# Six staging buffers and one weight piece per step in the expert stage of a fused attention and mixture-of-experts kernel

## Chip, cores and metric

The kernel runs on one core of a Trainium2 chip. Its time is the device time of one execution in microseconds (us), and the number to predict is the median over several executions. "Profile" means the page and the views made from one execution that the hardware profiler recorded.

## The reference, cut to what matters

Three stages follow each other. Attention with a running decay gives 2304 rows of 512 numbers. A dense feed-forward network works on them, and an expert stage on its result.

```python
scores = scale * q @ k.T + decay           # causal, 4 x 8 heads, S = 576, D = 64
x = softmax(scores) @ v                    # as 2304 x 512
h = x @ w_in                               # 512 -> 2048
x = maximum(0.01 * h, h) @ w_out           # 2048 -> 512
logits = x @ w_gate                        # 8 experts
# greedy over all logits in falling order: each token takes the first
# expert that still has room, each expert takes 2304 / 8 = 288 tokens
for e in range(8):
    h = maximum(x[mask[e]] @ w1[e], 0.0)   # 512 -> 1024
    out[mask[e]] = h @ w2[e]               # 1024 -> 512
```

## The kernel before, in words

**Products.** Every float32 product is made of three passes of a shorter format: a number is split into a high part (a cast) and a low part (the number less its high part), and high x high, low x high and high x low are added up in PSUM. So each operand costs a cast, mostly on ACT, and a subtraction on DVE or POOL before PE can use it. In the names, `h` at the end is a high part, `l` a low part: `gh` and `gl` for the hidden layer of the dense network, `eh` and `el` for that of an expert; `wh` stands for both parts of a weight.

**Stages.** Attention runs to about 300 us. The dense network's first product and half of its second follow, to about 438. Its second product, `deferred`, is put off: 9 groups of 256 tokens, each of 8 pieces of `g`, are multiplied from 438 on in the gaps of the routing, whose small steps (`r_...`, mostly on DVE) are one long dependent chain. `split_g` (L457, L458) splits a piece: the cast on ACT, the subtraction on POOL, and for the last group (number 8) the cast on ACT and the subtraction on DVE through helpers that keep the order of the program. After each group `leave_first` (L1012) copies the two sums `acc` to `xo`, which SP stores to `x2d` in memory. Rows for expert 0 are gathered there before the last group is finished; the rows that are missing then are added by products of the last sums `Y` with a selection matrix, in the PSUM banks `q_ct`, `q_base` and `q_misc`. `part_operand` (L1032, L1033) splits the result to `X0`, which the profile calls `XE`.

**Expert stage.** It begins at about 676.7. For each expert, `first` (L1172) makes one 128-row block of the hidden layer, 12 products of 128x288 into a bank `h3`; ACT makes `eh` (L1176) and DVE `el` (L1177). `after` (L1185) multiplies the block by a part of `w2`, 12 products into four banks `y`. One such step is j, and there are 8; block j+1 is made before the y products of step j. `turn` (L1163) transposes the gathered rows `xe` of the next expert into bank `T3` in four of the steps, and `leave` (L1192) transposes the result of the expert before, which POOL scatters to `out` with an indirect DMA (`send`, L1198).

**Weights.** An expert has 8 pieces of 512 KB: pieces 0 to 3 hold `w1`, pieces 4 to 7 `w2`. `split_weights` (L354 to L364) loads a piece with two DMAs on SP into a staging buffer `wst`, casts its two halves to `wh` and subtracts for the low parts. There are two staging buffers, and room for 10 split pieces (`WB` = 40 tiles). `fetch(e)` calls it for all 8 pieces of an expert, and is called for expert e+1 at the start of expert e. Pieces 0 to 3 of expert 0 are loaded during `deferred`.

**What sets the order.** A scheduler of the tile framework places the instructions of each engine from a simulated timeline, with the order of the program as its guide. Instructions through the lower-case helpers `vec`, `act`, `pe`, `gp`, `sp` (L74) are kept in program order on their engine, as are the y products of expert 0. All else, written with V, A, PE, G, may move.

**The end** (L1235 to L1240): the last result is transposed into four banks; 384 columns of each of three tiles are copied by DVE, ACT, DVE, and then DVE copies the last 128 columns of each, and POOL sends it.

Of the kernel before, what the change touches and what calls it, by code (L numbers as in the profile page):

```python
# [32 lines left out]
NC = DM // 128  # L33
# [13 lines left out]
FIN = ("act", "vec"), ("vec", "gp")  # L47
LAG = 3
AFTER = 1500, 800
WIDE1 = (0, 1), (2, 3), (4, 5), (6, 7), (8,)  # L50
# [179 lines left out]
def tile_kernel(ctx, tc, q, k, v, f, w_in, w_out, w_gate, w1, w2, out):  # L230
# [124 lines left out]

    def split_weights(pieces, lo_on, hi_on=A):
        st = wp.tile([128, 1024], FT, name="wst", tag="wst", bufs=2)
        for lo, hi, src in pieces:
            nc.sync.dma_start(st[:, lo:hi], src)
        r = []  # L360
        for u in range(2):
            r.append([wp.tile([128, 512], FR, name="wh", tag="w", bufs=WB) for _ in range(2)])
            x = st[:, 512 * u:512 * u + 512]
            hi_on.copy(r[u][0], x)  # L364
            lo_on.tensor_tensor(r[u][1], x, r[u][0], op=OP.subtract)
        return r
# [608 lines left out]
    def deferred(mm, last):  # L975

        for g in range(NG):
# [6 lines left out]
            def taken(half, i):  # L984
                if half:
                    x = gtp.tile([128, 2, GT], FT, name="g0", tag="g0", bufs=3)
                    nc.sync.dma_start(x, gd[g][:, 2 * i:2 * i + 2])
                else:
                    x = g1((g,), slice(2 * i, 2 * i + 2))[:, 0]
                return split_g(x, *((vec, act) if g == NG - 1 else (G, A)))  # L990
            ahead = []
# [45 lines left out]
    with ExitStack() as c2:  # L1037
# [95 lines left out]
        for t in range(2):  # L1133
            A.copy(Y[:, t, 0], last[t])
            V.tensor_tensor(Y[:, t, 1], last[t], Y[:, t, 0], op=OP.subtract)
        for l in range(2):
            for t in range(2):
                for c in range(NC):
                    mm(px[c][:, :CAP], Y[:, t, l, 128 * c:128 * c + 128], sel8[t], start=False, stop=l == t == 1)
# [5 lines left out]

    with ExitStack() as c3:
        ps = c3.enter_context(tc.tile_pool(name="ps3", bufs=1, reuse_waits="tile", space=PSUM))
        ep = c3.enter_context(tc.tile_pool(name="ep", bufs=1, reuse_waits="tile"))
        scat = []
        NJ = F2 // 128  # L1150

        def fetch(e):

            w = early if e == 0 else []
            for n in range(len(w) // 2, NC + NF // 2):
                w += split_weights(piece(e, n), vec, act if e == 0 and n < 6 else A)
            wa, wb = [w[:NC], w[NC:2 * NC]], w[2 * NC:]
            return wa, wb

        def turn(X, xe, c, own=False):  # L1160
            p = ps.tile([128, 512], FT, name="T3", tag="T3", bufs=2)
            for t in range(3):
                (pe if own else PE).transpose(p[:, M * t:M * t + M], xe[t][:, 128 * c:128 * c + 128], ident[:M, :M])  # L1163
            part_operand(X, c, p)

        def first(X, wa, j, own=False):
            h = ps.tile([128, 512], FT, name="h3", tag="h3", bufs=2)
            n = 0
            for x in range(2):
                for c in range(NC):  # L1170
                    for w in wa[j // 4][c][:2 - x]:
# [17 lines left out]
        def leave(e, ys, t):  # L1189
            p = ps.tile([128, 512], FT, name="T3", tag="T3", bufs=2)  # L1190
            for c in range(NC):
# [12 lines left out]
        def operand():  # L1204
            return ep.tile([128, NC, 2, CAP], FR, name="XE", tag="XE", bufs=2)
        W = {0: fetch(0)}
        xe = {}
# [3 lines left out]
        for e in range(E):  # L1211
            wb = W[e][1]
            if e + 1 < E:
                W[e + 1] = fetch(e + 1)
                xe[e + 1] = gather(e + 1, [ep.tile([M, DM], FT, name="xe", tag="xe", bufs=6) for _ in range(3)])
                X[e + 1] = operand()
            yt = [ps.tile([128, 512], FT, name="y", tag="y", bufs=NC) for _ in range(NC)]
            for j in range(NJ):
                for i in range(j, j + 2):
                    n, i = e + i // NJ, i % NJ  # L1220
                    if n < E and (n, i) not in g:
                        g[n, i] = first(X[n], W[n][0], i, e == 0)
                after(yt, wb, j, *g[e, j], e == E - 1, e == 0)
                if ys and j < 3:
# [5 lines left out]
            for c in range(NC):  # L1230
                (A.copy if c % 2 else V.tensor_copy)(ys[:, c], yt[c][:, :CAP])
        p = [ps.tile([128, 512], FT, name=n, tag=n, bufs=2) for n in ("T3", "T3", "h3", "h3")]
        for c in range(NC):
# [3 lines left out]
        for t in range(3):  # L1237
            (A.copy if t % 2 else V.tensor_copy)(yo[t][:, :384], p[t][:M, :384])
        for t in range(3):
            V.tensor_copy(yo[t][:, 384:], p[3][:M, 128 * t:128 * t + 128])  # L1240
            send(E - 1, yo[t], t)
# [226 lines left out]
```

## Time and profile before

| | |
|---|---|
| median of 3 runs | 921.39 us (920.62 to 921.4) |
| the profiled execution | 920.77 us, span of the trace 918.7 us |
| PE busy | 882.8 us, 96% of the span, 6916 instructions |
| DVE, POOL, ACT busy | 584.6, 440.3, 415.7 us |
| costliest group of PE | `acc` products of `deferred`, 185.5 us for 576 of them |
| `h` and `y` products of the experts with high parts | 101.1 us for 660, 100.8 us for 512 |
| casts of weights on ACT in the expert stage | 75.9 us for 124, with 80.9 us of idle time before them, most of it behind loads of `wst` |

Times in the trace count from the start of the span. A row gives a start, a duration and an instruction, `x` a count, and in brackets how long its engine stood idle before it and what ended that. An engine's idle time matters only where that engine, at that point, sets when the next work ends. The granted clock is TensorE's: 1.00 is its upper level of 2.4 GHz, about 0.5 the lower one of 1.2 GHz.

### The profile page before, as it was taken

The numbers are of one execution on the slowest core, as the hardware profiler recorded it, in microseconds if no ns is written. First come the engines' busy times: TensorE is split into PE (matmuls) and PEld (weight loads), VectorE is DVE, ScalarE is ACT, GpSimd is POOL, SyncE is SP. The second block draws the span as 40 slices with busy tenths as digits, with TensorE's granted clock in tenths as the row PEclk, the third lists the DMA queues.
The fourth block names the chain that finished last, engine by engine and source line by source line (L and its number), as shares of the span: only waits on it lengthen the run. The fifth ranks groups of instructions, "written<-read, shape, count | busy, mean of one in ns | idle before, by whom it ended". The sixth has DMA issues, their size and how long they took to land.

```text
span 918.7 us, 19048 instructions
## 1 busy us (share of the span) xinstructions
PE 882.8 (96%) x6916; PEld 751.6 (82%) x6916; DVE 584.6 (64%) x1458; ACT 415.7 (45%) x984; POOL 440.3 (48%) x670
## 2 busy tenths in 40 slices
PE   6899999999999999999999999999997999999996
PEld 6688878878878887776777777777787999999995
DVE  8778876517798379324867667776546665656631
ACT  7999999842223233314122222221345455555521
POOL 8588895548998078002656555554121122121111
PEclk9899999999999999999999999999999999999998
DMA  6566654559984485402321212212166665655601
GB/s 129 150 166 169 182 131 128 174 155 360 326 272 149 143 261 170 136 25 69 116 71 46 68 60 69 69 47 70 54 195 201 191 195 174 200 191 187 200 28 35
DMA packets 139965, 132.34 MB, mean 144 GB/s; under 512 B 68480, under 2 KB 106688, under 8 KB 139872
## 3 DMA queue, kind: packets, MB, share of 16 engines
q1 hardware_dynamic: 135600, 121.40, 43.1%
q0 software_dynamic: 3072, 9.44, 3.5%
q8 instruction: 54, 0.88, 0.4%
q10 hardware_dynamic: 1200, 0.30, 0.2%
q14 instruction: 39, 0.32, 0.1%
HBM read 99.84 MB, written 31.08 MB: 143 GB/s over the span
## 4 chain that ended last, share of the span: by engine, by line
PE 77%; POOL 7%; ACT 5%; DVE 3%; DMA 3%; issue 2%; POOLq 0%; SPq 0%; DVEq 0%; ACTq 0%
PE acc L1095 21%; PE h L74 11%; PE acc L74 11%; PE y L1185 10%; PE h L1172 10%; PE s L74 6%; PE T L74 3%; ACT kept L74 3%; DMA wst<-in_moe_w 2%; PE q_ct L1095 2%; POOL ln L74 2%; POOL wsq L74 2%; POOL P L74 1%; PE T L1192 1%; DVE r_ge L1346 1%
## 5 line engine op out<-in xcount | busy, mean ns | idle before, releaser
L1095 PE MATMUL acc<-wh,gh 128*128 128x512 f32 x576 | 185.5, 399 | 1.2 <-ACT gh L74 1.2
L458 POOL TENSOR_TENSOR gl<-g,gh 128x512 fp32r<-128x512 f32 x64 | 106.9, 1676 | 75.5 <-ACT gh L457 69.8
L74 DVE TENSOR_TENSOR wh<-wst,wh 128x512 fp32r<-128x512 f32 x144 | 99.0, 707 | 48.9 <-ACT wh L364 38.0
L1095 PEld LDWEIGHTS acc<-wh,gh 128*128 128x128 f32 x576 | 106.1, 189 | 20.3 <-ACT gh L74 1.6
L1095 PE MATMUL acc<-wh,gl 128*128 128x512 f32 x288 | 115.6, 402 | 1.3 <-POOL gl L458 1.3
L364 ACT CAST wh<-wst 128x512 fp32r<-128x512 f32 x124 | 75.9, 620 | 80.9 <-DMA wst<-in_moe_w 59.5
L74 PE MATMUL h<-X,wh 128*128 128x512 f32 (+1 forms) x480 | 104.2, 374 | 0.6 <-DVE xt L74 0.6
L74 PE MATMUL acc<-X,wh 128*128 128x512 f32 (+1 forms) x480 | 104.5, 374 | 0.0
L457 ACT CAST gh<-g 128x512 fp32r<-128x512 f32 x64 | 39.5, 621 | 142.8 <-PE acc L1095 120.4
L1172 PE MATMUL h<-XE,wh 128*128 128x288 f32 x660 | 101.1, 301 | 2.6 <-DVE el L1177 2.6
L1185 PE MATMUL y<-eh,wh 128*128 128x288 f32 x512 | 100.8, 297 | 2.7 <-ACT eh L1176 2.7
L74 PEld LDWEIGHTS h<-X,wh 128*128 128x128 f32 x480 | 82.5, 188 | 18.2 <-issue 1.0
L74 PEld LDWEIGHTS acc<-X,wh 128*128 128x128 f32 x480 | 82.3, 188 | 18.4 <-DVE g L74 1.7
L1172 PEld LDWEIGHTS h<-XE,wh 128*128 128x128 f32 x660 | 90.3, 189 | 2.8 <-DVE el L1177 2.8
L74 ACT ACTIVATE kept<-kept,nm 128x192 f32<-128x192 f32 (+4 forms) x160 | 88.0, 553 | 3.1 <-DVE nm L74 3.1
L1198 POOL DMA_INDIRECT out<-yo,ids x24 | 24.0, 1002 | 127.6 <-DVE yo L1194 103.9
L1185 PEld LDWEIGHTS y<-eh,wh 128*128 128x128 f32 x512 | 81.0, 189 | 3.2 <-ACT eh L1176 3.2
L74 DVE SCALAR_TENSOR_TENSOR wbits<-w,wbits 128x256 int32<-128x256 int32 x128 | 73.3, 575 | 2.3
L74 DVE CUSTOM_DVE_ANT_0 kept<-s,mask 128x192 f32<-128x192 f32 (+4 forms) x160 | 59.2, 426 | 22.7 <-PE s L74 22.0
L1185 PE MATMUL y<-el,wh 128*128 128x288 f32 x256 | 70.5, 299 | 0.5 <-DVE el L1177 0.5
L1027 POOL DMA_INDIRECT xe<-x2d,ids x24 | 26.1, 1089 | 93.6 <-PE T L1163 34.8
L74 POOL TENSOR_TENSOR wst<-wsq,wbits 128x256 f32<-128x256 f32 x64 | 50.6, 791 | 33.0 <-DVE wbits L74 28.2
(245 smaller groups left out, 1731.4 us busy)
## 6 DMA issues: line engine op xcount, KB each, us to landing
wst<-in_moe_w SPq DMA_DIRECT2D x128, 256.0 KB
X<-xd SPq DMA_DIRECT2D x12, 1024.0 KB
g<-gd SPq DMA_DIRECT2D x36, 256.0 KB
w<-in_moe_w_in SPq DMA_DIRECT2D x32, 256.0 KB
w<-in_moe_w_out SPq DMA_DIRECT2D x32, 256.0 KB
gd<-g SPq DMA_DIRECT2D x16, 512.0 KB
xd<-xt SPq DMA_DIRECT2D x16, 320.0 KB
x2d<-xo SPq DMA_DIRECT2D x20, 256.0 KB
```

The source lines that it names most:

```text
L74: r = getattr(self.engine, name)(*a, **k)
L364: hi_on.copy(r[u][0], x)
L457: hi_on.copy(gh, g)
L458: on.tensor_tensor(gl, g, gh, op=OP.subtract)
L1027: G.indirect_dma_start(out=x, out_offset=None, in_=x2d[:, :], in_offset=bass.IndirectOffsetOnAxis(ap=ids[:, 3 * e + t:3 * e + t + 1], axis=0))
L1095: tc.keep_in_program_order(PE.matmul(*a, **k))
L1172: (pe if own else PE).matmul(h[:, :CAP], w[:, 128 * (j % 4):128 * (j % 4) + 128], X[:, c, x, :], start=n == 0, stop=n == 3 * NC - 1)
L1185: o = PE.matmul(yt[c][:, :CAP], w[:, s], a, start=j == 0 and n == 0, stop=j == NJ - 1 and n == 2)
L1192: PE.transpose(p[:M, 128 * c:128 * c + 128], ys[:, c, M * t:M * t + M], ident)
L1198: sd = G.indirect_dma_start(out=out[:, :], out_offset=bass.IndirectOffsetOnAxis(ap=ids[:, 3 * e + t:3 * e + t + 1], axis=0), in_=y, in_off ...
L1346: V.scalar_tensor_tensor(many[:, :NT * (K + 1)].rearrange("p (i k) -> p i k", k=K + 1)[:, :, :K], key[:, :, None].to_broadcast(s), base if ...
```

## The change

1. `split_weights` takes a room: with one, the piece is staged in one of `NWS` = 6 buffers `ws` of the experts' own pool. Only pieces 4 and 5 of expert 0 still use `wst`.
2. `fetch` becomes `more(e, n)`, one piece, called once in every inner step: an expert's own pieces 6 and 7 in its steps 0 and 1, the next expert's pieces 0 to 5 in steps 2 to 7. All casts and subtractions keep the order of the program.
3. The PSUM pool of the experts becomes three, with `h3` first. `h3` so lies in banks of the last `acc`, and no longer in those of `q_ct`.
4. In `deferred`, the first two pieces of the last group are split by instructions that may move. The very first piece of group 0 has its low part made on DVE, not on POOL.
5. The products with `Y` go tile by tile instead of high parts first.
6. At the end each tile's copies stand together, and ACT makes the 384-column copies of two tiles.

```diff
+NWS = 6
...
-    def split_weights(pieces, lo_on, hi_on=A):
-        st = wp.tile([128, 1024], FT, name="wst", tag="wst", bufs=2)
+    def split_weights(pieces, lo_on, hi_on=A, room=None):
+        st = room.tile([128, 1024], FT, name="ws", tag="ws", bufs=NWS) if room else wp.tile([128, 1024], FT, name="wst", tag="wst", bufs=2)
...
-                return split_g(x, *((vec, act) if g == NG - 1 else (G, A)))
+                n = NF // 2 * half + i
+                return split_g(x, *((vec, act) if g == NG - 1 and n > 1 else (V if g == NG - 1 or g == n == 0 else G, A)))
...
-        for l in range(2):
-            for t in range(2):
+        for t in range(2):
+            for l in range(2):
                 for c in range(NC):
                     mm(px[c][:, :CAP], Y[:, t, l, 128 * c:128 * c + 128], sel8[t], start=False, stop=l == t == 1)
...
+        psh = c3.enter_context(tc.tile_pool(name="ps3h", bufs=1, reuse_waits="tile", space=PSUM))
+        pst = c3.enter_context(tc.tile_pool(name="ps3t", bufs=1, reuse_waits="tile", space=PSUM))
         ps = c3.enter_context(tc.tile_pool(name="ps3", bufs=1, reuse_waits="tile", space=PSUM))
...
-        def fetch(e):
-
-            w = early if e == 0 else []
-            for n in range(len(w) // 2, NC + NF // 2):
-                w += split_weights(piece(e, n), vec, act if e == 0 and n < 6 else A)
-            wa, wb = [w[:NC], w[NC:2 * NC]], w[2 * NC:]
-            return wa, wb
+        def more(e, n):
+
+            if e < E:
+                W.setdefault(e, []).extend(split_weights(piece(e, n), vec, act, None if e == 0 and n < 6 else ep))
...
-            h = ps.tile([128, 512], FT, name="h3", tag="h3", bufs=2)
+            h = psh.tile([128, 512], FT, name="h3", tag="h3", bufs=2)
...
-        W = {0: fetch(0)}
+        W = {0: early}
+        for n in (4, 5):
+            more(0, n)
...
-                W[e + 1] = fetch(e + 1)
...
-                after(yt, wb, j, *g[e, j], e == E - 1, e == 0)
+                more(e + (j > 1), (j + 6) % 8)
+                after(yt, W[e][2 * NC:], j, *g[e, j], e == E - 1, e == 0)
...
         for t in range(3):
-            (A.copy if t % 2 else V.tensor_copy)(yo[t][:, :384], p[t][:M, :384])
-        for t in range(3):
+            (A.copy if t else V.tensor_copy)(yo[t][:, :384], p[t][:M, :384])
             V.tensor_copy(yo[t][:, 384:], p[3][:M, 128 * t:128 * t + 128])
             send(E - 1, yo[t], t)
```

How the instructions move, at three places. Lines of the changed kernel are one or two higher than before.

ACT at the start of expert 0, before: `XE` is the operand of expert 0, `h_...` are the blocks of its hidden layer in turn.

```order
L1032 CAST XE_8796<-q_misc 128x288
L74 CAST wh<-wst 128x512 x3
L1176 ACTIVATE eh<-h_9087 128x288
L364 CAST wh<-wst 128x512 x2
L1176 ACTIVATE eh<-h_9104 128x288
L364 CAST wh<-wst 128x512 x2
L1176 ACTIVATE eh<-h_9133 128x288
L364 CAST wh<-wst 128x512 x4
L1176 ACTIVATE eh<-h_9162 128x288
```

The same place after the change:

```order
L1034 CAST XE_8796<-q_misc 128x288
L75 CAST wh<-wst 128x512 x2
L1177 ACTIVATE eh<-h_8983 128x288
L75 CAST wh<-wst 128x512
L1177 ACTIVATE eh<-h_9000 128x288
L75 CAST wh<-ws 128x512 x2
L1177 ACTIVATE eh<-h_9040 128x288
L75 CAST wh<-ws 128x512 x2
L1177 ACTIVATE eh<-h_9080 128x288
```

Two casts of weights, never more, now stand ahead of an `eh`, and from the third block on they read `ws`. On SP the loads of `ws` stand where those of `wst` stood, behind the two stores of `x2d`.

DVE at the start of the deferred product (group 0), before: `W_5071` are the logits, `r_...` the first steps of the routing.

```order
L1267 TENSOR_REDUCE r_m<-W_5071 128x18
L1293 TENSOR_TENSOR r_tru<-r_on,r_tri 128x128
L1320 TENSOR_TENSOR r_eq<-W_5071,r_m 128x144
L1333 TENSOR_SCALAR r_k_6219<-r_m 128x18
L1321 TENSOR_TENSOR r_eq<-r_eq,r_we 128x144
L1334 TENSOR_TENSOR r_k_6219<-r_m,r_k_6219 128x18
L1267 TENSOR_REDUCE r_mw<-r_eq 128x18
```

The same place after the change:

```order
L1268 TENSOR_REDUCE r_m<-W_5071 128x18
L1294 TENSOR_TENSOR r_tru<-r_on,r_tri 128x128
L1321 TENSOR_TENSOR r_eq<-W_5071,r_m 128x144
L459 TENSOR_TENSOR gl<-g_5108,gh 128x512
L1334 TENSOR_SCALAR r_k_6219<-r_m 128x18
L1322 TENSOR_TENSOR r_eq<-r_eq,r_we 128x144
L1335 TENSOR_TENSOR r_k_6219<-r_m,r_k_6219 128x18
```

The low part `gl` of group 0's first piece has come in behind two routing steps; on POOL, where it was the first of that group, it is gone.

ACT at group 8, before: `xo` are the copies of group 7's sums, the `gh` of L74 the pieces of group 8, `r_ge` a late step of the routing.

```order
L457 CAST gh<-g_8610 128x512
L457 CAST gh<-g_8628 128x512
L1012 COPY xo<-acc 128x512 x2
L74 CAST gh<-g_5949 128x512 x4
L1430 ACTIVATE r_ge<-r_ga,r_ip 128x18x24
```

The same place after the change:

```order
L458 CAST gh<-g_8628 128x512
L458 CAST gh<-g_5949 128x512 x2
L1014 COPY xo<-acc 128x512
L75 CAST gh<-g_5949 128x512
L1014 COPY xo<-acc 128x512
L75 CAST gh<-g_5949 128x512
L1431 ACTIVATE r_ge<-r_ga,r_ip 128x18x24
```

The first pieces of group 8 now stand ahead of the two copies and between them.

## Rows read from the trace of the kernel before

**Rows 1.** The page's chain that ended last: shares of the span by engine.

```profile
PE 77%; POOL 7%; ACT 5%; DVE 3%; DMA 3%; issue 2%; POOLq 0%; SPq 0%; DVEq 0%; ACTq 0%
```

**Rows 2.** Windows of the expert stage: window, length, busy time and count of PE, PEld, DVE, ACT, POOL, then granted clock, DMA share, GB/s.

```profile
676.74:715.27 38.53, 32.79 (x215) 31.33 (x216) 21.11 (x38) 18.01 (x36) 8.79 (x9) 0.91 0.70 209
743.50:910.00 166.50, 166.08 (x1285) 165.72 (x1283) 93.38 (x176) 78.21 (x167) 28.32 (x27) 1.00 0.49 155
```

**Rows 3.** Chain of waits: first `h` products of experts 2 and 7 (start, time, line).

```profile
743.55 2.78 PE h L1172 x21
883.03 2.78 PE h L1172 x21
```

**Rows 4.** Timeline of PE, expert 0: start, us, what, count, [idle before <-releaser].

```profile
676.74 3.46 PE L74 MATMUL h<-XE,wh 128*128 128x288 f32 x24 [1.16 <-DVE XE L1033]
693.55 0.53 PE L1185 MATMUL y<-eh,wh 128*128 128x288 f32 x2 [2.12 <-ACT eh L1176]
696.31 0.68 PE L74 MATMUL T<-ident,xe 96*128 96x96 f32 x3
711.51 1.32 PE L1172 MATMUL h<-XE,wh 128*128 128x288 f32 x6 [2.56 <-DVE el L1177]
```

**Rows 5.** Windows behind three waits of PE, columns as in group 2.

```profile
440.00:441.00 1.00, 1.00 (x4) 0.83 (x5) 1.00 (x1) 0.00 (x0) 1.00 (x1) 1.00 0.99 334
695.00:698.40 3.40, 3.40 (x17) 3.38 (x17) 1.75 (x3) 2.11 (x4) 0.00 (x0) 0.51 0.65 207
712.00:715.20 3.20, 3.20 (x16) 3.20 (x15) 0.00 (x0) 0.00 (x0) 0.00 (x0) 0.52 0.81 215
```

**Rows 6.** Timeline of ACT before the first long wait.

```profile
691.27 1.92 ACT L364 CAST wh<-wst 128x512 fp32r<-128x512 f32 x3 [1.77 <-DMA wst<-in_moe_w]
693.10 0.40 ACT L1176 ACTIVATE eh<-h 128x288 fp32r<-128x288 f32 x1
```

**Rows 7.** Timeline of SP at expert 0, and its waits (times: us, count, longest).

```profile
678.64 54.66 SPq L359 DMA_DIRECT2D wst<-in_moe_w  x36
SPq L359 <- DVE wh L74: 39.8, 20, 10.0
```

**Rows 8.** DMA from 680 to 689; landing of the gathers into `xe`.

```profile
DMA packets 1207, 2.66 MB, mean 295 GB/s; under 512 B 183, under 2 KB 183, under 8 KB 1205
DMA to landing us min/median/max: 3.3/4.8/6.9
```

**Rows 9.** Timeline of DVE: the last low part of expert 0's operand.

```profile
676.97 0.45 DVE L1033 TENSOR_TENSOR XE<-q_misc,XE 128x288 fp32r<-128x288 f32 x1
```

**Rows 10.** Timeline of ACT at group 8.

```profile
644.96 1.26 ACT L1012 COPY xo<-acc 128x512 f32<-128x512 f32 x2 [7.35 <-PE acc L1095]
```

**Rows 11.** Timeline of PE at group 8.

```profile
645.21 0.39 PE L1095 MATMUL acc<-wh,gl 128*128 128x512 f32 x1
646.79 0.73 PE L1095 MATMUL acc<-wh,gh 128*128 128x512 f32 x2 [1.19 <-ACT gh L74]
```

**Rows 12.** Timelines of PE and POOL at group 0.

```profile
439.97 0.50 PE L1095 MATMUL acc<-wh,gl 128*128 128x512 f32 x1 [1.30 <-POOL gl L458]
438.64 3.84 POOL L458 TENSOR_TENSOR gl<-g,gh 128x512 fp32r<-128x512 f32 x3
```

**Rows 13.** Timeline of DVE at group 0; `r_eq` elsewhere (min/median/max, ns); a `gl` of DVE.

```profile
438.82 1.18 DVE L1293 TENSOR_TENSOR r_tru<-r_on,r_tri 128x128 bf16<-128x128 bf16 x1
439.92 1.40 DVE L1320 TENSOR_TENSOR r_eq<-W,r_m 128x144 f32<-128x144 f32 x1
L1320 DVE TENSOR_TENSOR r_eq<-r_W,r_m x7: 296/299/1400, 469.1 to 640.3; 128x144 f32<-128x144 f32 x7
650.94 0.69 DVE L74 TENSOR_TENSOR gl<-g,gh 128x512 fp32r<-128x512 f32 x1
```

**Rows 14.** Timelines of DVE and POOL at the end.

```profile
910.01 0.67 DVE L1240 COPY yo<-h 96x128 f32<-96x128 f32 x3
911.79 0.92 POOL L1198 DMA_INDIRECT out<-yo,ids  x1 [0.30 <-issue]
```

More of the change, by code (lines that the diff above doesn't have):

```diff
@@ L1150, in tile_kernel @@
         NJ = F2 // 128
-        def fetch(e):
-            w = early if e == 0 else []
-            for n in range(len(w) // 2, NC + NF // 2):
-                w += split_weights(piece(e, n), vec, act if e == 0 and n < 6 else A)
-            wa, wb = [w[:NC], w[NC:2 * NC]], w[2 * NC:]
-            return wa, wb
+        def more(e, n):
+            if e < E:
+                W.setdefault(e, []).extend(split_weights(piece(e, n), vec, act, None if e == 0 and n < 6 else ep))
         def turn(X, xe, c, own=False):
-            p = ps.tile([128, 512], FT, name="T3", tag="T3", bufs=2)
+            p = pst.tile([128, 512], FT, name="T3", tag="T3", bufs=2)
             for t in range(3):
@@ L1170, in first @@
                 for c in range(NC):
-                    for w in wa[j // 4][c][:2 - x]:
+                    for w in wa[NC * (j // 4) + c][:2 - x]:
                         (pe if own else PE).matmul(h[:, :CAP], w[:, 128 * (j % 4):128 * (j % 4) + 128], X[:, c, x, :], start=n == 0, stop=n == 3 * NC - 1)
@@ L1189, in leave @@
         def leave(e, ys, t):
-            p = ps.tile([128, 512], FT, name="T3", tag="T3", bufs=2)
+            p = pst.tile([128, 512], FT, name="T3", tag="T3", bufs=2)
             for c in range(NC):
@@ L1211, in tile_kernel @@
         for e in range(E):
-            wb = W[e][1]
             if e + 1 < E:
-                W[e + 1] = fetch(e + 1)
                 xe[e + 1] = gather(e + 1, [ep.tile([M, DM], FT, name="xe", tag="xe", bufs=6) for _ in range(3)])
@@ L1221, in tile_kernel @@
                     if n < E and (n, i) not in g:
-                        g[n, i] = first(X[n], W[n][0], i, e == 0)
-                after(yt, wb, j, *g[e, j], e == E - 1, e == 0)
+                        g[n, i] = first(X[n], W[n], i, e == 0)
+                more(e + (j > 1), (j + 6) % 8)
+                after(yt, W[e][2 * NC:], j, *g[e, j], e == E - 1, e == 0)
                 if ys and j < 3:
@@ L1231, in tile_kernel @@
                 (A.copy if c % 2 else V.tensor_copy)(ys[:, c], yt[c][:, :CAP])
-        p = [ps.tile([128, 512], FT, name=n, tag=n, bufs=2) for n in ("T3", "T3", "h3", "h3")]
+        p = [x.tile([128, 512], FT, name=n, tag=n, bufs=2) for n, x in (("T3", pst), ("T3", pst), ("h3", psh), ("h3", psh))]
         for c in range(NC):
```

## The prediction

> **What bounds the kernel now.** I read the chain of waits first, then the windows by stage, then the timelines of single engines at the places where PE stood still. Three quarters of the chain is PE [rows 1], so the end moves only where PE's idle or slowed time goes or grows. Of the windows of the expert stage, the one from 743.50 has PE busy for 166.08 of 166.50 us at granted clock 1.00 [rows 2]. Experts 1 to 7 are therefore bound by PE, and nothing can be won there. Their period is (883.03 - 743.55) / 5 = 27.90 us [rows 3]. An expert has 192 products of 128x288 and 24 transposes; with 2.1 us for the transposes (an estimate) a product takes (27.9 - 2.1) / 192 = 0.134 us.
>
> Expert 0 is different. From its first product at 676.74 [rows 4] to the first of its last y products at 715.27 lie 38.53 us with 215 PE instructions (203 products, 12 transposes) at a mean clock of 0.91 [rows 2]. At the later rate 203 products take 27.3 us, with 0.8 for the transposes (an estimate) 28.1. So **10.4 us are lost in expert 0**. PE was idle for 38.53 - 32.79 = 5.74 of them, 2.12 behind an `eh` of ACT and 2.56 behind an `el` of DVE [rows 4]. The other 4.7 is time in which PE was busy but slow: after each of these two waits the granted clock is 0.51 and 0.52, the lower of its two levels (1.2 GHz), for 3.4 and 3.2 us [rows 5].
>
> Why is `eh` late? ACT has three casts of weights in a row ahead of it, and these wait 1.77 us for a weight load [rows 6]. The loads are late because there are two staging buffers: SP issues 36 of them in one stretch of 54.66 us, and 39.8 us of its waits are for DVE's subtraction, the last reader of a buffer [rows 7]. So the weights of expert 1 cannot be fetched ahead, and their casts stand on ACT in front of work for expert 0.
>
> **The change, part by part.**
>
> *Staging and order of casts.* Six buffers instead of two, and at most one piece (four casts in all, two on ACT, two on DVE) per inner step. The order on ACT shows it: never more than two casts ahead of an `eh`, where four stood. An inner step of PE takes 27.9 / 8 = 3.5 us; a step's ACT work is two casts at 0.64 (1.92 / 3) and one `eh` of 0.40 [rows 6], some 1.7 us, with an XE cast beside them in four of the steps. So ACT keeps up if the loads come. They do: eight pieces of 0.52 MB and three gathers of 0.20 MB per expert are 4.8 MB; at the 295 GB/s that the queues moved at their busiest here [rows 8] that is 16 us of 28. In expert 0 POOL issues nine gathers (the x9 of its window [rows 2]), which makes 6.0 MB and 20 us, still under 28. SP passes its two `x2d` stores first, as before, then issues six pieces: twelve loads, 3.1 MB, beside the gathers. Expert 1's three gathers are issued by 681.26 and land after 3.3 to 6.9 us today [rows 8]; their first transpose comes at 696.31 now [rows 4], and some 3 us sooner without the first stall. That leaves 5 us of room. I take the whole 10.4 less 0.2 for steps in which an XE cast stands beside two weight casts: **-10.2**. Bounds: -10.4, and 0 if loads alone set the pace.
>
> The gathers and the loads are on different queues, q0 and q1 of the page, and were in flight together while the gathers landed in 3.3 to 6.9 us [rows 8]. The Trainium skill, "DMA: Bandwidth & Descriptors", section "Queues, rings and completion order", says that a DMA engine goes round its queues packet by packet; by it a gather waits for its turn and not for all twelve loads, and the sum holds the whole -10.2. Strictly in order of issue it would hold some -5.5, which is rival C below. No row here shows twelve loads in flight beside a gather.
>
> *Other PSUM banks.* `h3` now takes the banks of the last `acc` and not those of `q_ct`, so the first product need not wait for the readers of `q_ct`. Before, PE waits 1.16 us for DVE's XE [rows 4]; but the high parts that its first eight products need do not hang on those readers, and DVE's last low part ends at 676.97 + 0.45 = 677.42 [rows 9]. Started early, the first block still waits for that last operand: its end moves from 676.74 + 12 x 0.134 = 678.3 to some 0.2 us behind 677.42, **-0.7**. Bounds 0 and -1.2 (all of the wait).
>
> *Group 8.* The first two pieces of the last group of the deferred product are cast out of the order kept by hand, so that on ACT `gh` stands ahead of the copies `xo`. Now the two `xo` run from 644.96 for 1.26 us [rows 10] ahead of the `gh`, and PE waits 1.19 us for it at 646.79 after a product that starts at 645.21 [rows 11]. With the overlap that products in a row have (0.16 us, an estimate) that makes **-1.35**. Bounds 0 and -1.35. The `xo` copies go later by the casts' 1.2 us; their banks are wanted a whole group later.
>
> *Group 0.* Here the change adds a wait. The low part of the first piece goes from POOL to DVE, where the order shows it behind `r_tru` and `r_eq`. POOL's `gl` of 438.64 takes 3.84 / 3 = 1.28 us and releases PE at 439.97 [rows 12]. DVE starts `r_tru` at 438.82 and `r_eq` at 439.92; this `r_eq` takes 1.40 us where the same operation has a median of 0.30 [rows 13]. Both end where a `gl` of POOL ends (438.64 + 1.28 = 439.92, + 2.56 = 441.20). POOL still has two `gl` to do from 438.64 on, so I take the stretch as staying: DVE's `gl` starts at about 441.25 and takes 0.69 [rows 13], PE resumes at about 442.0: **+2.05**. Its wait is then 1.30 + 2.05 = 3.35 us. The wait of 1.30 us left the clock at 1.00, those of 2.12 and 2.56 were followed by half the clock for 3.2 and 3.4 us [rows 5]; so I add half of that, **+1.6**. Bounds: +0.1 if nothing is stretched (438.82 + 2 x 0.30 + 0.69 = 440.1) and +3.65.
>
> The Trainium skill, "SBUF — State Buffer", section "Who interferes with whom", says that a VectorE instruction with two SBUF inputs and a GpSimd one that reads SBUF shut each other out for a whole instruction. By that rule the sum holds the +2.05; by the unstretched rows alone it would hold +0.1. The 1.40 beside 0.30 agrees with the rule.
>
> *Y products in another order.* PE's short wait for a cast of `Y` may go; what follows is set by ACT's `xo` copies and XE casts and DVE's low parts to 677.42 [rows 9], which PE 0.2 us earlier does not move. Taken as 0; without that cover it would be -0.2 at most.
>
> *Tail.* Now DVE does two copies of 384 columns and then, from 910.01, three of 128 [rows 14], and the first send on POOL waits for the first of these. With each 128-column copy right behind its tile's, the first send starts about 0.45 us earlier; the sends run 0.92 + 0.30 = 1.22 apart [rows 14] and set the end: **-0.45**. Bounds 0 and -0.6.
>
> Sum: -10.2 - 0.7 - 1.35 - 0.45 + 2.05 + 1.6 = **-9.05**. The profiled execution took 920.77, 0.62 under the median of 921.39 of the runs shown; 920.77 - 9.05 = 911.7, as a median **912.3**.
>
> **The rivals.** The sum, as it stands, is case A, with 910.7 to 914 as its own range (the small terms at their bounds).
>
> B, group 0 is cheaper: without the fall of the clock 912.3 - 1.6 = 910.7; with nothing stretched 912.3 - 3.65 = 908.6. For it: the other row that is stretched, `r_tru`, has no unstretched twin, so the price rests on one row. Against: it ends with POOL's `gl` as `r_eq` does.
>
> C, one stall stays in expert 0: gathers or loads come behind the twelve loads, and one of the two waits is still there. It would cost half of what both cost, (2.12 + 2.56) / 2 + 4.7 / 2 = 4.7: 917.0. For it: 3.1 MB at once takes 10.5 us at 295 GB/s, so a gather that had to wait for all of it would land at about 692, and the transposes wait for it. Against: the gathers landed within 6.9 us while the queues were full [rows 8].
>
> Same: the loads are bound by DMA after all, expert 0 keeps its 10.4 us, and the other parts, -2.5 and +3.65, nearly cancel: 921.39 + 1.15 = 922.5. For it: the queues are at 295 GB/s from 680 to 689 [rows 8]. Against: the windows have them at 209 GB/s over expert 0 and 155 after it [rows 2].
>
> D, slower: pieces 6 and 7 of an expert are now cast in its own steps 0 and 1, not during the expert before. If their load and cast take longer than the four steps until `y` wants piece 6 (4 x 3.5 = 14 us), PE stops once in every expert from 1 on: 7 x 4.7 = 33 more, 945. For it: the slack in front of the later pieces was a whole expert, and is half of one now. Against: with six buffers the load is issued four or five steps before its cast, and such loads and gathers need 3.3 to 6.9 us.
>
> **How the numbers follow.** A 0.50, B 0.20, C 0.20, same 0.05, D 0.05. The likeliest is A, 912.3. The range goes from B's lower end, 908.6, to C's 917.0 and leaves same and D out. The measurement of this kernel can tell 0.2%, 1.8 us, from nothing: A, B and C lie under 919.5, so faster 0.90; same 0.05; slower 0.05.
>
> **What would show it.** In the profile after, PE should have no wait above 0.5 us in expert 0, the clock there should read 1.00 throughout, and from its first `h` to its first y product of the last step should be some 28 us; SP should show waits for `ws` buffers on casts one step at a time. PE at group 0 should wait 3.3 us for DVE's `gl`, with a clock near 0.5 behind it; at group 8 no wait for `gh`. Wrong would be the forecast if `eh` of expert 0 still waited behind a DMA (C), if a wait came back once every 28 us (D), or if the clock stayed up at 442 (B).

## The result, and the profile after

The changed kernel took 915.60 us at the median of 9 runs (912.11 to 919.41), the kernel before 921.83 us at the median of 9 runs of the same series. The ratio of the two is 0.9918, with a 95% interval of 0.9902 to 0.9933. A second series, on another occasion, gave 912.05 us (910.72 to 913.67, 6 runs) against 923.42 us: ratio 0.9883 (0.9860 to 0.9906). The forecast was 912.3 us, a ratio of 0.990, with a range of 908.6 to 917.0. The profiled execution of the first series took 912.11 us, its span is 910.4 us; it was the fastest of its nine.

The page of the changed kernel, engines and chain (columns as on the page of before, its chain in [rows 1]):

```profile
PE 879.4 (97%) x6916; PEld 749.8 (82%) x6916; DVE 586.1 (64%) x1458; ACT 413.2 (45%) x985; POOL 432.7 (48%) x669
...
PE 85%; DVE 5%; POOL 4%; ACT 2%; issue 2%; DMA 1%; SPq 0%; POOLq 0%; DVEq 0%; ACTq 0%
```

PE's share of the chain rose from 77% to 85%, and the loads are nearly gone from it. Next the timeline of PE at group 0 and in expert 0, and the windows there:

```profile
440.74 0.79 PE L1097 MATMUL acc<-wh,gl 128*128 128x512 f32 x1 [3.28 <-DVE gl L459]
...
677.25 3.57 PE L75 MATMUL h<-XE,wh 128*128 128x288 f32 x24 [0.64 <-ACT XE L1034]
...
688.36 0.53 PE L1186 MATMUL y<-eh,wh 128*128 128x288 f32 x2 [0.96 <-ACT eh L1177]
```

```profile
677.25:707.20 29.95, 28.99 (x216) 28.39 (x217) 18.04 (x34) 14.38 (x32) 7.77 (x9) 1.00 0.85 271
...
441.00:442.00 1.00, 1.00 (x3) 0.81 (x4) 1.00 (x8) 0.00 (x0) 0.00 (x0) 0.50 0.98 296
442.00:443.00 1.00, 1.00 (x3) 0.75 (x3) 1.00 (x2) 0.00 (x0) 0.00 (x0) 0.50 0.97 333
443.00:444.00 1.00, 1.00 (x4) 0.77 (x3) 1.00 (x1) 0.00 (x0) 0.00 (x0) 0.52 0.01 2
```

These answer to [rows 2, 4, 12]. The two long waits of expert 0 are gone, its clock is 1.00 throughout, and the same 203 products and 12 transposes take 29.95 us where they took 38.53. At group 0 PE now waits 3.28 us, with half the clock behind it. At group 8 no wait is left.

To see where the time went, I cut each traced execution into five stretches at points that PE passes in all kernels: A from the start to the first `gh` product of group 0, B from there to the end of the last product with `Y`, C PE's wait for expert 0, D from the first `h` to the last 24 `y` products, E from those to the end of the span. (Starts and ends are read from PE's timelines and chains, the span as printed, to a tenth; this table is worked out, not printed by the profiler. Its rows below the difference are the experiments of the next section.)

```
us                      A        B       C      D       E      span
before               437.96   237.62   1.16   228.35   13.61   918.7
changed              436.74   239.87   0.64   219.85   13.30   910.4
difference            -1.22    +2.25  -0.52    -8.50   -0.31   -8.30
a1_change_again      436.63   241.08   0.64   218.42   13.23   910.0
e1_group0_on_pool    438.87   236.97   0.64   218.42   13.30   908.2
e1_again             437.00   236.55   0.63   218.42   13.30   905.9
e2_staging_alone     438.22   238.48   1.17   218.20   13.63   909.7
e3_two_buffers       437.67   238.26   0.65   218.41   13.21   908.2
e4_all_at_start      438.62   238.26   0.64   218.58   13.20   909.3
e8_three_on_dve      440.30   236.49   0.64   218.43   13.24   909.1
e9_pool_free         437.83   240.43   0.64   218.42   13.28   910.6
e10_order_alone      438.16   240.88   0.64   219.85   13.27   912.8
e11_two_at_start     436.53   241.23   0.64   223.96   13.24   915.6
e12_no_staging_part  438.21   239.95   0.64   226.81   13.29   918.9
```

Stretch A lies ahead of everything that the change touches, and it differs by up to 3.8 us from one execution to the next (436.53 to 440.30), by 1.9 us between two traces of one and the same program (438.87 and 437.00). So I do not count 1.22 us of the 8.30 as the change's. C, D and E repeat to a tenth or two where the programs agree there, but for the one late instruction in D that the next section comes to. B does not: before and with the staging part alone, which changes nothing in it, B differs by 0.86 us. Some 19 us into it a step of the routing on DVE, `r_ge`, and a `gl` of POOL start within 0.01 us of each other. POOL and DVE in the trace of before, then with the staging part alone:

```profile
456.81 3.70 POOL L458 TENSOR_TENSOR gl<-g,gh 128x512 fp32r<-128x512 f32 x1 [3.28 <-ACT gh L457]
456.82 2.54 DVE L1346 SCALAR_TENSOR_TENSOR r_ge<-r_k,r_step 128x2286 bf16<-128x2286 f32 x1
...
457.08 1.28 POOL L459 TENSOR_TENSOR gl<-g,gh 128x512 fp32r<-128x512 f32 x1 [3.28 <-ACT gh L458]
457.09 3.68 DVE L1345 SCALAR_TENSOR_TENSOR r_ge<-r_k,r_step 128x2286 bf16<-128x2286 f32 x1
```

In the trace of before it was `gl` that took longer; in the twelve others it was `r_ge`, and PE waited 0.76 us for it. There is only one trace of before, and measured against it B looks 0.86 us worse than it is.

### The profile page after: what moved, and what is told of

Same layout as the page of the kernel before. It is cut to its first block, busy times and chain, and to the rows that moved or that the text cites. A ratio compares the mean times of both kernels' runs of the same rounds, so it can differ in the third digit from the quotient of the medians.

```text
span 910.4 us, 18988 instructions
## 1 busy us (share of the span) xinstructions
PE 879.4 (97%) x6916; PEld 749.8 (82%) x6916; DVE 586.1 (64%) x1458; ACT 413.2 (45%) x985; POOL 432.7 (48%) x669
## 4 chain that ended last, share of the span: by engine, by line
PE 85%; DVE 5%; POOL 4%; ACT 2%; issue 2%; DMA 1%; SPq 0%; POOLq 0%; DVEq 0%; ACTq 0%
PE acc L1097 21%; PE h L75 13%; PE acc L75 11%; PE y L1186 11%; PE s L75 10%; PE h L1173 10%; PE T L75 4%; PE q_ct L1097 2%; DVE kept L75 2%; ACT kept L75 1%; DVE r_ge L1347 1%; PE T L1193 1%; POOL ln L75 1%; DMA w<-in_moe_w_in 1%; POOL P L75 1%
## 5 line engine op out<-in xcount | busy, mean ns | idle before, releaser
L459 POOL TENSOR_TENSOR gl<-g,gh 128x512 fp32r<-128x512 f32 x63 | 102.3, 1626 | 84.5 <-ACT gh L458 77.3
L1186 PE MATMUL y<-eh,wh 128*128 128x288 f32 x512 | 104.4, 297 | 1.0 <-ACT eh L1177 1.0
L1178 DVE SCALAR_TENSOR_TENSOR el<-h,eh 128x288 fp32r<-128x288 f32 x64 | 29.3, 457 | 75.3 <-ACT eh L1177 75.3
L75 DVE TENSOR_TENSOR wh<-ws,wh 128x512 fp32r<-128x512 f32 x116 | 75.6, 687 | 2.4
L1186 PE MATMUL y<-el,wh 128*128 128x288 f32 x256 | 74.8, 298 | 0.0
L1177 ACT ACTIVATE eh<-h 128x288 fp32r<-128x288 f32 x64 | 26.3, 411 | 91.7 <-PE h L1173 79.3
```

Source lines behind the costliest of these rows:

```text
L75: r = getattr(self.engine, name)(*a, **k)
L459: on.tensor_tensor(gl, g, gh, op=OP.subtract)
L1186: o = PE.matmul(yt[c][:, :CAP], w[:, s], a, start=j == 0 and n == 0, stop=j == NJ - 1 and n == 2)
```

## The experiments

**The changed kernel once more**, no edit.

> The changed kernel once more, unchanged, for a second trace of it. If the forecast's steps are what the first trace shows, PE again waits 3.1 to 3.5 us for DVE's gl at group 0, with the clock at about half for some 3.3 us behind it, and expert 0 takes 29 to 31 us from its first h to the first y product of its last step. The first trace also had a wait of 0.96 us in expert 0 behind an eh whose products were done 3.7 us earlier: if something fixed in the program holds ACT there, the same eh is late again by 2 us or more; if it is chance, that wait is gone or stands elsewhere. The time should be 7 to 8 us under the kernel before.

Measured 912.05 us, 11.4 us under the median of before in its series and not the 7 to 8 expected. Of its trace, the window of expert 0, PE's first product after the wait of group 0, the third `eh` on ACT, and the window behind the wait; then the third `eh` of the first trace:

```profile
678.35:706.87 28.52, 28.52 (x216) 28.36 (x217) 18.22 (x34) 14.49 (x32) 8.10 (x9) 1.00 0.91 284
...
440.63 0.80 PE L1097 MATMUL acc<-wh,gl 128*128 128x512 f32 x1 [3.28 <-DVE gl L459]
...
685.35 0.41 ACT L1177 ACTIVATE eh<-h 128x288 fp32r<-128x288 f32 x1 [1.95 <-PE h L75]
...
440.63:447.60 6.97, 6.97 (x18) 5.50 (x19) 3.71 (x10) 0.62 (x1) 1.65 (x2) 0.56 0.32 103
```

```profile
681.17 1.14 ACT L75 CAST wh<-ws 128x512 fp32r<-128x512 f32 x2
687.90 0.41 ACT L1177 ACTIVATE eh<-h 128x288 fp32r<-128x288 f32 x1 [5.59 <-PE h L75]
```

Without a wait, expert 0 takes 28.52 us, less than the 29 to 31 expected. The wait of group 0 is there again, but the mean clock of 0.56 over 6.97 us means that it stayed low for some 6 us, not 3.3. In the first trace the third `eh` started at 687.90 though its products had ended at about 684.2, and ACT had nothing else to do; that cost 219.85 - 218.42 = 1.43 us of stretch D. It is not always there.

**Group 0's first piece back on POOL.**

```diff
-... (V if g == NG - 1 or g == n == 0 else G, A)
+... (V if g == NG - 1 else G, A)
```

> Only group 0's first low part goes back to POOL. Theory (DVE's two routing steps in front are stretched by POOL, and the long wait halves the clock): the wait of PE falls from 3.28 us to about 1.3 us, the clock behind it stays at 1.00, and the time is 3.4 us (3.0 to 3.8) under the changed kernel. Rival 1 (the wait costs, the clock fall would have come anyway): 2.0 us under it. Rival 2 (POOL, with one piece more ahead of the others, is late with the next pieces): no gain, within 0.5 us.

Measured 909.76 us (909.28 to 911.39), ratio to before 0.9859 (0.9831 to 0.9887): 2.3 us under the changed kernel of the same series. Timelines of POOL and PE:

```profile
439.55 3.83 POOL L459 TENSOR_TENSOR gl<-g,gh 128x512 fp32r<-128x512 f32 x3
...
440.87 0.50 PE L1097 MATMUL acc<-wh,gl 128*128 128x512 f32 x1 [1.28 <-POOL gl L459]
```

The wait is 1.28 us again, and a first product of 0.50 us, not 0.80, shows a clock that has not fallen. Stretch B falls by 4.1 us against the repeat and 2.9 against the first trace. The wait and the clock came out as the theory said. The time did not: 2.3 us is under its 3.0 to 3.8 and nearer to rival 1's 2.0. The run without a clock fall below (two buffers) has B at 238.26, 1.3 to 1.7 us over the two traces with the piece on POOL (236.97, 236.55), so the wait alone is worth that much, and the clock comes on top only in the executions in which it falls.

**The staging part alone**, on the kernel before: `split_weights` with a room, `more`, and its calls.

> The kernel before with the six staging buffers and one piece per step alone; PSUM banks, groups 0 and 8, order of Y and tail as before. Theory (the staging carries nearly all of the gain): expert 0 takes 29 to 31 us from its first h to the first y product of its last step, and the time is 8 to 9 us under the kernel before, about 1 us under the changed kernel, since the loss at group 0 (3.4) is larger than the gain of the small parts (2). Rival (the new PSUM banks or the order around the start of expert 0 are needed too): 4 to 6 us under the kernel before.

Measured 910.71 us, ratio 0.9869 (0.9845 to 0.9892): 12.7 us under the median of before, more than either theory said. Its window of expert 0, and the waits at group 8 and at the start of expert 0 that the other parts were to remove:

```profile
677.87:706.17 28.30, 28.30 (x215) 28.26 (x216) 17.57 (x32) 13.64 (x29) 7.90 (x9) 1.00 0.90 278
...
647.92 0.73 PE L1096 MATMUL acc<-wh,gh 128*128 128x512 f32 x2 [1.19 <-ACT gh L75]
...
677.87 3.45 PE L75 MATMUL h<-XE,wh 128*128 128x288 f32 x24 [1.17 <-DVE XE L1034]
```

By stretches it is plainer: D falls by 228.35 - 218.20 = 10.15 us, nearly all of the 10.4 that were to be had, while C (1.17) and E (13.63) stay as before. The staging part carries the gain alone. The span of this execution is 9.0 us under that of before (909.7 and 918.7); why the medians lie 12.7 apart is open.

**Two buffers in place of six**, in the changed kernel.

```diff
-NWS = 6
+NWS = 2
```

> The changed kernel with two staging buffers in the experts' pool, not six; the order of the instructions stays. Theory (depth): the loads come late again, expert 0 has at least one wait of 2 us with a clock fall behind it, 4 to 9 us over the changed kernel. Rival (order): one piece per step asks for a load every 3.5 us, two buffers keep up with that, the waits in expert 0 stay under 1 us and the time is within 1 us of the changed kernel.

Measured 912.66 us, ratio 0.9892, 0.6 us over the changed kernel. Stretch D is 218.41 us, the same to the hundredth as with six, and PE has no wait in expert 0. The rival holds: with one piece asked for per step, depth is worth nothing. The trace also shows a wait at group 0 with no fall of the clock (PE, and the window behind it):

```profile
441.67 0.50 PE L1097 MATMUL acc<-wh,gl 128*128 128x512 f32 x1 [3.28 <-DVE gl L459]
...
442.00:444.00 2.00, 2.00 (x10) 1.67 (x9) 2.00 (x8) 0.00 (x0) 0.00 (x0) 1.00 0.93 321
```

**Six buffers, but all pieces asked for at the start of the expert, casts free to move.**

```diff
-                W.setdefault(e, []).extend(split_weights(piece(e, n), vec, act, None if e == 0 and n < 6 else ep))
+                W.setdefault(e, []).extend(split_weights(piece(e, n), vec, act if e == 0 and n < 6 else A, None if e == 0 and n < 6 else ep))
...
             if e + 1 < E:
+                for n in range(8):
+                    more(e + 1, n)
...
-                more(e + (j > 1), (j + 6) % 8)
```

Not shown: at the start all four missing pieces of expert 0 are asked for, not two.

> The changed kernel with its six buffers, but with all eight pieces of the next expert asked for at the expert's start and their casts free to move, as before the change: two to four casts stand ahead of an eh in expert 0 again. Theory (after the run with two buffers: the order of the casts is what counts, not the depth): with six buffers the loads are there early, so the casts ahead of an eh run without a wait for a load, but three or four of them take 1.9 to 2.5 us, and PE waits 0.5 to 2 us at one or two steps of expert 0; 1 to 5 us over the changed kernel. Rival (either depth or order is enough): expert 0 has no wait over 0.3 us, within 1 us of the changed kernel. Rival 2 (depth is worth nothing): the full 10 us of expert 0 come back.

Measured 912.03 us, ratio 0.9879. Expert 0 in its trace, and a cast on ACT right ahead of an `eh`:

```profile
677.52:706.37 28.85, 28.78 (x215) 28.38 (x216) 21.26 (x40) 18.43 (x39) 9.33 (x9) 1.00 1.03 336
...
691.84 0.62 ACT L365 CAST wh<-ws 128x512 fp32r<-128x512 f32 x1 [1.24 <-DMA ws<-in_moe_w]
```

28.85 us, 0.07 of it idle, with three or four casts ahead of an `eh` as before the change. My theory (a few waits of 0.5 to 2 us from the casts alone) fell; the first rival holds. So depth alone is enough too. It does not take away every wait of a cast for its load: several are left, the longest single one ahead of an `eh` of expert 0 is 1.24 us. They are short enough that PE never waits.

**Order with the old two buffers; two new buffers without the order; the staging part undone.** Three kernels that part order from depth: the first stages all pieces in `wst`; the second is the last kernel with `NWS = 2`; the third is the last kernel with all pieces in `wst`.

```diff
-... split_weights(piece(e, n), vec, act, None if e == 0 and n < 6 else ep)
+... split_weights(piece(e, n), vec, act)
```

> The changed kernel with one piece per step and the casts in order, but staged in the old two buffers; the new ones are gone. Theory (either the order or more buffers is enough): a piece is asked for every 3.5 us and a buffer comes free with each step, so the waits in expert 0 stay under 1 us and the time is within 1.5 us of the changed kernel. Rival (two more buffers were the cure in the run with two new ones, since four are there at the start of expert 0): a wait of 2 us or more and a clock fall come back in expert 0, 4 to 9 us over the changed kernel.

> Two new buffers, and all pieces of the next expert asked for at the expert's start with free casts, the rest as changed. Theory (with casts that are free to move the depth must hide the loads): with two buffers the loads are late as in the kernel before, casts that wait for loads stand ahead of an eh, expert 0 has a wait of 1.5 us or more and takes 36 to 39 us from its first h to the first y product of its last step (29 in the changed kernel); 6 to 11 us over the changed kernel. Rival (the two more buffers at the start of expert 0 are what counts, whatever the order): no wait over 0.5 us, within 1 us of the changed kernel.

> The changed kernel without the staging part: old two buffers, all pieces asked for at the expert's start, casts free to move. It holds the other parts (banks, groups 0 and 8, Y, tail). Theory: expert 0 takes 38 to 39 us again, and the time is 9 to 10 us over the changed kernel, about that of the kernel before or up to 2 us over it, since the loss at group 0 (3.4) is larger than the gain of the other parts (2). Rival (the banks or the start of expert 0 share in the gain): 4 to 6 us over the changed kernel.

Measured in one series: 914.58 us, ratio 0.9901 (0.9867 to 0.9934); 917.78 us, ratio 0.9944 (0.9916 to 0.9972); 920.97 us, ratio 0.9967 (0.9948 to 0.9987). Stretch D in that order: 219.85, 223.96, 226.81 us. ACT and PE of the order alone, then ACT and PE of two new buffers, then PE with the staging part undone:

```profile
686.07 0.62 ACT L75 CAST wh<-wst 128x512 fp32r<-128x512 f32 x1 [2.38 <-DMA wst<-in_moe_w]
...
690.32 0.41 ACT L1177 ACTIVATE eh<-h 128x288 fp32r<-128x288 f32 x1 [2.77 <-PE h L75]
...
690.78 0.53 PE L1186 MATMUL y<-eh,wh 128*128 128x288 f32 x2 [0.94 <-ACT eh L1177]
```

```profile
691.58 0.62 ACT L365 CAST wh<-ws 128x512 fp32r<-128x512 f32 x1 [2.61 <-DMA ws<-in_moe_w]
692.10 0.40 ACT L1177 ACTIVATE eh<-h 128x288 fp32r<-128x288 f32 x1
...
696.16 0.62 ACT L365 CAST wh<-ws 128x512 fp32r<-128x512 f32 x1 [2.08 <-DMA ws<-in_moe_w]
...
711.10 0.93 PE L75 MATMUL h<-XE,wh 128*128 128x288 f32 x5 [1.62 <-issue]
```

```profile
689.88 0.53 PE L1186 MATMUL y<-eh,wh 128*128 128x288 f32 x2 [0.92 <-ACT eh L1177]
...
701.51 0.54 PE L1186 MATMUL y<-eh,wh 128*128 128x288 f32 x2 [0.86 <-ACT eh L1177]
...
710.67 0.93 PE L75 MATMUL h<-XE,wh 128*128 128x288 f32 x5 [1.19 <-ACT XE L1034]
...
732.12 1.19 PE L1186 MATMUL y<-eh,wh 128*128 128x288 f32 x7 [1.06 <-ACT eh L1177]
```

With the order alone ACT's casts do wait for loads (2.38 us), but there is one piece in front of an `eh`, so PE's only wait of over 0.3 us in expert 0 is 0.94, at the third `eh`, the same one that was late in the first trace, and it costs the same 1.43 us. By the ratios (0.9901 and 0.9883) the time is 1.7 us over the repeat, about the 1.5 of the theory. Without the order two buffers are not enough: the cast that waits 2.61 us for its load stands right ahead of the `eh`, as in [rows 6]. PE waits 0.80 us for that `eh`, and 1.62 us at a product for which the profile names no cause; expert 0 takes 34.3 us and not 36 to 39, and by the ratios the time is 5.6 us over the repeat, a little less than the 6 to 11 of the theory.

With the staging part undone D is 8.4 us over that of the repeat, and the ratio to before is 0.8% over it: the other parts do not bring the gain. The theory was right in this and missed twice: expert 0 takes 33.4 us and not 38 to 39 (the last of the four waits shown is in expert 1), and the time is 3.0 us under that of before, not equal to it or over it. PE's waits in D are no shorter in sum than before (6.1 and 5.7 us), but none of them was followed by a fall of the clock, as two were before [rows 5]; I take that as the reason for 226.81 in place of 228.35.

**Three low parts of group 0 on DVE.**

```diff
-... (V if g == NG - 1 or g == n == 0 else G, A)
+... (V if g == NG - 1 or g == 0 and n < 3 else G, A)
```

> The changed kernel with the low parts of group 0's first three pieces all on DVE, so that POOL has no gl while DVE makes r_tru, r_eq and the first gl. Theory (POOL's gl hold DVE's two-input steps up): r_tru and r_eq take 0.2 to 0.4 us each, not 1.18 and 1.38, the first gl ends some 1.3 us after PE's last product, PE waits 1.1 to 1.5 us, and the clock does not fall: 3 to 4 us under the changed kernel, about as the run with the piece on POOL. Rival (DVE is slow there for a reason of its own): r_eq stays at 1.4 us and the wait at 3.3 us.

Measured 909.47 us, ratio 0.9851 (0.9835 to 0.9868). DVE of the first trace of the changed kernel, then DVE and PE of this one:

```profile
437.60 1.18 DVE L1294 TENSOR_TENSOR r_tru<-r_on,r_tri 128x128 bf16<-128x128 bf16 x1
438.70 1.38 DVE L1321 TENSOR_TENSOR r_eq<-W,r_m 128x144 f32<-128x144 f32 x1
440.00 0.68 DVE L459 TENSOR_TENSOR gl<-g,gh 128x512 fp32r<-128x512 f32 x1
```

```profile
441.15 0.22 DVE L1294 TENSOR_TENSOR r_tru<-r_on,r_tri 128x128 bf16<-128x128 bf16 x1
441.28 0.30 DVE L1321 TENSOR_TENSOR r_eq<-W,r_m 128x144 f32<-128x144 f32 x1
441.50 0.69 DVE L459 TENSOR_TENSOR gl<-g,gh 128x512 fp32r<-128x512 f32 x1
...
442.25 0.50 PE L1097 MATMUL acc<-wh,gl 128*128 128x512 f32 x1 [1.23 <-DVE gl L459]
```

With no `gl` on POOL, `r_tru` takes 0.22 us and not 1.18, `r_eq` 0.30 and not 1.38, and PE waits 1.23 us. Theory shown: POOL's `gl` held DVE's steps up. It was never that DVE is the slower engine for this piece (0.69 us here, 1.28 on POOL).

**POOL emptied ahead of group 0**, with the piece on POOL.

```diff
-                early.extend(split_weights(piece(0, g - 3), G))
+                early.extend(split_weights(piece(0, g - 3), vec))
```

> The kernel with group 0's first piece back on POOL, and besides with the low parts of expert 0's first two weight pieces made on DVE later, in the program's order; on POOL they ran just ahead of group 0's gl for 5 us. Theory (POOL's queue is why the first gl is late): POOL makes the first gl right behind its gh, PE's wait at group 0 falls from 1.28 us to under 0.3 us, and the time is 1 to 1.5 us under the run with the piece on POOL. Rival (the four subtractions on DVE delay the routing, which PE follows): a new wait of PE behind a routing step, within 0.5 us of it or over it.

Measured 912.86 us, ratio 0.9896 (0.9880 to 0.9913), 4.1 us over the run with the piece on POOL in the same series (908.77 us). POOL, DVE and PE:

```profile
438.22 3.97 POOL L459 TENSOR_TENSOR gl<-g,gh 128x512 fp32r<-128x512 f32 x3 [2.95 <-DVE W L75]
...
516.77 3.45 DVE L75 TENSOR_TENSOR wh<-wst,wh 128x512 fp32r<-128x512 f32 x2
...
520.55 0.16 PE L1097 MATMUL q_base<-r_found,r_rows 128*128 128x1 bf16 x1 [2.00 <-DVE r_found L1357]
```

My theory fell. POOL stood idle for 2.95 us and began `gl` 0.39 us behind PE's first `gh` product, where it was 0.68 us (439.55 - 438.87) with the full queue; the wait fell from 1.28 to 0.99 us only. So its queue is worth 0.29 us of the 1.28, and not nearly all of it. In the program this `gl` waits for PE's last transpose of the logits `L`; that it lies in the memory of `L` is my reading of that wait, and was not tried. And the subtractions on DVE held a routing step up, for which PE waited 2.00 us, twice. The rival holds, and was worse than it said.

**The piece on POOL once more.**

> The kernel with group 0's first piece back on POOL once more, beside the last one on the same chip: 1.28 us of wait at group 0, 13 to 14 us under the kernel before.

Measured 908.77 us (907.91 to 908.92), ratio 0.9847 (0.9830 to 0.9863), 14.3 us under the median of before, with a wait of 1.29 us at group 0. This version, the change without its edit at group 0, is the fastest of all that ran, and its interval lies under that of the changed kernel in the second series (0.9860 to 0.9906) but for 0.0003.

## Why the prediction was right

- **Staging, -10.2.** Measured in stretch D: -8.50 in the first trace, of which one late `eh` took 1.43, and -9.93 in the repeat; -10.15 with the staging part alone. The size was right. The reason was half right: the prediction named buffers and order together, and the runs show that either of them does it. Order with two new buffers gives D = 218.41, with the old ones 219.85 and the late `eh` in it; six buffers without the order 218.58; neither, 223.96 with four buffers in all and 226.81 with two. Casts that wait for loads ahead of an `eh` are left with the order alone (2.38 us) and with the depth alone (1.24 us), and cost PE nothing that can be seen. In the repeat the third `eh` starts at 685.35, takes 0.41 us, and PE's first product with it comes at 688.35; so an `eh` may be some 2.6 us late (an estimate from these three numbers) before PE stands still. What has to go is a delay longer than that.
- **The loads, and rival C.** The stall of rival C did not come. The reason given against it did not hold, though: the gathers were slowed by the loads. Landing of the six gathers that are issued beside loads of expert 0, before, in the repeat, and with two buffers:

```profile
DMA to landing us min/median/max: 3.7/5.4/6.9
...
DMA to landing us min/median/max: 5.8/9.0/9.1
...
DMA to landing us min/median/max: 4.3/4.9/5.9
```

In the repeat the last gather of expert 1 is issued at 682.79 and so lands by 691.9, and the first transpose of its rows begins at 693.14: 1.3 us of room, where the prediction counted 5. From 684 to 692 the loads moved 1.54 MB and the gathers 0.88. That both move at once agrees with what the Trainium skill, "DMA: Bandwidth & Descriptors", section "Queues, rings and completion order", says of turns between queues. But a gather among many loads took longer here than a gather among few.
- **Rival D.** Fell. Two of the pieces of `h` in the chain of the changed kernel, one expert apart:

```profile
735.43 2.39 PE h L1173 x18
...
763.36 2.38 PE h L1173 x18
```

27.93 us, as in [rows 3]: pieces 6 and 7, cast in their own expert, are in time.
- **Group 0, +2.05 and +1.6.** The wait was forecast as 3.35 us and measured as 3.28 or 3.29 in seven traces that hold the edit, 1.98 over that of before. Its cause was shown by the run with three pieces on DVE. The Trainium skill, "SBUF — State Buffer", section "Who interferes with whom", has the rule, and the 0.30 us beside 1.38 agrees. The clock term is no fixed cost: behind the same wait the clock stayed up in two traces (B = 238.26), fell for some 3 us in the first (239.87), later in one (239.95) and for about 6 us in three (240.88 to 241.23). That is 0 to 3 us. The forecast's 1.6, half a fall as a guess, is met by the first trace and by the mean of the seven (1.7), but the first trace and the repeat, the same kernel, gave 1.6 and 2.8.
- **Group 8, -1.35.** The wait of 1.19 us is gone in each trace with the edit. From the first product of group 7 to that of group 8 PE takes 27.25 us in the trace of before and 27.23 with the staging part alone, and 25.86 to 25.90 in the eleven traces with the edit: -1.35, as forecast.
- **Banks, -0.7.** PE's wait fell by 0.52 us only, from 1.16 to 0.64, and the first 24 products grew from 3.46 [rows 4] to 3.57. But the products with `Y`, now in another order, also ended 0.33 us sooner, which lengthens that wait. From the start of the last `acc` product, before and after,

```profile
672.66 0.39 PE L1095 MATMUL acc<-wh,gl 128*128 128x512 f32 x1
...
674.02 0.39 PE L1097 MATMUL acc<-wh,gl 128*128 128x512 f32 x1
```

to the end of those 24 products it is 7.54 and 6.80 us: -0.74, as forecast. What released PE is ACT's first XE cast; no run parts the banks from the order of `Y`. **Tail, -0.45:** -0.31 in E, -0.3 to -0.4 in the others.
- **The sum.** Without stretch A the first trace gives -7.1 and the repeat -7.4 (B +3.46, C -0.52, D -9.93, E -0.38) against the forecast -9.05. Of what is missing, 2.0 and 1.7, the late `eh` is 1.43 in the first trace, the longer fall of the clock 1.2 in the repeat, and 0.86 in both is the `r_ge` that was not held up in the one trace of before. With these set right both come to some -9.4, so the terms of the sum hold.
- **The range.** The median of the first series, 915.60, lies outside the 910.7 to 914 that the sum was given for itself. It is inside the range only because that was drawn out to rival C's 917.0, and rival C's stall did not come; that is luck. The second series, 912.05, lies where the sum put it. That the first median stood 3.5 us over its profiled execution was not foreseen. Causes seen in traces (stretch A, the clock at group 0, the late `eh`) are large enough for it; which of them it was in those runs is open.

## What to carry to other kernels

When casts of prefetched weights share an in-order engine with work on the critical path, first look at what stands in front of that work in the queue: asking for one piece per step, in program order, brought here about what six buffers brought, for no memory (stretch D within 1.4 us, the late `eh` included). More loads in flight also slow the transfers beside them, so look at what else uses the queues at that time. Before a step is moved to another engine, look at what that engine runs just ahead of it and whether the first engine, still busy with its neighbours, will slow that down. And before a small gain is read from one trace, cut the span into stretches: here the part ahead of the change alone varied by 3.8 us, and one race between two engines moved a later part by 0.86.

## What was not expected of the hardware

The same wait of 3.28 us was followed by a full clock, by about 3 us at half clock, or by about 6 us of it, with nothing in the program to tell these traces apart. And one `eh` of ACT, the third of expert 0, started late in three traces of thirteen (the first of the changed kernel, the order alone, the staging part undone), by 2 us and more, with its products done, the casts ahead of it finished, and no wait of its own in the program but the one for PE. In all three PE then waited 0.92 to 0.96 us. (With two new buffers ACT stood 2.35 us at the cast right behind that `eh`, with no releaser that the profile knows.) It is always this place of ACT's program, which speaks against a load as its cause.

What sets these four traces apart is that they have gaps. The first trace of the changed kernel holds 12034 records of semaphore events, the repeat of the same kernel 12379; in the first 10 us of expert 0 they hold 89 and 209. The other three are short in the same way (12017 to 12083 in all, 78 to 98 in these 10 us), and the nine traces without a late start are not (12371 to 12492, and 165 to 228). So the late start may come with the recording of an execution and not with the kernel. Whether the gap and the late start cause each other, or have one cause, no run here tells. What the profile names as releaser of an instruction in that stretch of these four traces is less sure than elsewhere; the starts and durations do not hang on it.
